# Block attention feeding a mixture of experts: keys scaled on GpSimd, TensorE's step grouped by kind of product, three PSUM banks each for scores and transposes

## The chip, the core and the metric

The kernel runs on one core of a Trainium2 chip. The metric is the device time of one execution in microseconds (us), given as the median of three runs. The profiler also recorded one execution with every instruction's start and duration; its span is counted from its first to its last instruction. In its rows PE is TensorE (PEld its weight loads), DVE is VectorE, ACT is ScalarE, POOL is GpSimd, and SPq is the queue on which SyncE issues DMA transfers.

## What is computed

Two stages follow each other. The first is attention with a window and block summaries (4 batches, 8 heads, 768 rows, head size 64), the second a mixture of 8 experts with the best two of them for each of the 3072 rows. Cut from the reference:

```python
k_sum = k.reshape(B, H, nb, block, D).max(axis=3)      # block 32: 24 summaries
v_sum = v.reshape(B, H, nb, block, D).mean(axis=3)
scores_l = scale * np.matmul(q, k.transpose(0, 1, 3, 2))   # scale = 1/8
scores_l_m = np.where(np.abs(pos[:, None] - pos[None, :]) < 16, scores_l, -1e9)
scores_s = scale * np.einsum('bhsd,bhnd->bhsn', q, k_sum) + np.log(block)
a = softmax(concatenate([scores_l_m, scores_s]))           # maximum taken off first
x = a @ concatenate([v, v_sum])                            # then [3072, 512]
noisy = x @ w_gate + log1p(exp(x @ w_noise)) * noise       # best two experts, softmax
out[row] += weight * (relu(x[row] @ w1[e]) @ w2[e])
```

## The kernel before

Attention goes over 24 tiles of 128 query rows (4 batches of 6 tiles; `t` is the tile). A tile's 128 rows are two blocks of 64, and each block needs 96 window keys plus the 24 block maxima, 120 keys in all. The 8 heads of a tile are split by partition half: `a` is the half (0 or 1), `hp` the four heads in it. The names of a tile's stages are:

- `kx_local` (L125) and `kx_sum` (L130): GpSimd copies the window keys (two copies of 128x384) and the block maxima into `kx`, the keys that TensorE reads. For the first tile `first_keys` (L238, L240) does this head by head.
- `mask_sums` (L315): four matmuls put the mask into the score tile `s`, and `scores` (L325): 32 matmuls add the products of `q` and `kx` to it. `s` has 2 buffers of 2 PSUM banks each, one bank for each half `a`.
- `smax` (L332): VectorE takes the maximum of each row and head. ScalarE makes its negative eighth, `nm` (L337), in a small copy.
- `sexp` (L339): eight exponentials on ScalarE, one for each head, four for each half `a`, with `nm` as bias and 0.125 as scale. The result is `p`.
- `p_trans` (L345): TensorE transposes `p`, four heads into each of the 2 banks `pt`; ScalarE copies each bank to `pts` (L348).
- `av` (L358): 32 matmuls of `pts` with the values give `o`; `norm` (L367, L371, L373) divides on VectorE and gives `x`.
- `x_pe` (L395): four transposes of `x` into `pt`, copied by ScalarE to `xt` (L401). `norm_hi` (L380, ScalarE) and `norm_lo` (L387, GpSimd) split `x` into two f16 parts that go to DRAM (`xd`).

The loop `for t in range(-2, NT - 1)` writes the instructions out in a pipelined order, and each engine works through its own list in that order. One turn holds the scores of tile t+2, the transposes of `p` of tile t+1, the `av` of tile t and the `x` of tile t-1. Some turns carry more: sums of the values (L266), the gate's products (L413, L424, L484 and on, L593), transfers, weight conversions (L686, L688). At a change of batch there is also the reduction of the keys to maxima (L231). Waits between engines are semaphore waits that the language derives from which tile each instruction reads and writes; the program that is built shows on which instruction each of them stands.

After the last tile (about 140 us into the span) the experts run: two large products (L871, L990), which fill TensorE to the end.

Of the kernel before, what the change touches and what calls it, by code (L numbers as in the profile page):

```python
# [20 lines left out]
P = 128  # L21
# [36 lines left out]
BIG = 1.5 * 2 ** 23  # L58


@with_exitstack
def attn_moe(ctx, tc, qt, kt, vt, wgn, noise, w1, w2, out):
# [10 lines left out]
    pairs = spair.enter_context(tc.tile_pool(name="pairs", bufs=2, space=PSUM))  # L73
# [45 lines left out]
    def kx_local(t):  # L119
        b, j = divmod(t, TS)  # L120
        for blk in range(2):
            c = j * P + 64 * blk
            r = max(0, c + W - S)
            k = KB[b % 2][:, r:r + HP * S].rearrange("p (h s) -> p h s", h=HP)
            nc.gpsimd.tensor_copy(KX[t % QN][:, :, blk, 0:W], k[:, :, c - r:c - r + W])  # L125

    def kx_sum(t):
        b, j = divmod(t, TS)
        if j < QN:
            (nc.gpsimd if b else nc.vector).tensor_copy(KX[t % QN][:, :, :, W:NK],  # L130
                                                        KM[b][:, :, None, :].to_broadcast([P, HP, 2, NB]))
# [102 lines left out]
    def first_keys():  # L234
        for h in range(HP):
            k = KB[0][:, h * S:]
            for blk in range(2):
                nc.gpsimd.tensor_copy(KX[0][:, h, blk, 0:W], k[:, 64 * blk:64 * blk + W])  # L238
            k_piece(0, h, 2 if h == HP - 1 else 1)
            nc.vector.tensor_copy(KX[0][:, h, :, W:NK], KM[0][:, h, None, :].to_broadcast([P, 2, NB]))  # L240
# [9 lines left out]
    C4 = 2 * (D + 1)  # L250

# [48 lines left out]
    SC, PE_, PT, PO, X, XR, XT = {}, {}, {}, {}, {}, {}, {}  # L300

    def gate_space():
        return pairs.tile([P, 2, 512], F32, name="s")
# [4 lines left out]
    def mask_sums(t):  # L308
        j = t % TS
        s = SC[t] = gate_space()[:, :, :SK].rearrange("p a (h k) -> p a h k", h=HP)  # L310
        for blk in range(2):
            for a in range(2):
                r = slice(64 * a, 64 * a + 64)
                m = masks[1 if (j, blk) == (0, 0) else 2 if (j, blk) == (TS - 1, 1) else 0]
                nc.tensor.matmul(s[64 * blk:64 * blk + 64, a, :, 0:W], identb[r, r],  # L315
                                 m[r, None, :].to_broadcast([64, HP, W]), start=True, stop=False,
                                 skip_group_check=True)

    def scores(t):
        s, q, k = SC[t], QR[t], KX[t % QN]  # L320
        for hp in range(HP):
            for blk in range(2):
                for a in range(2):
                    d = slice(64 * a, 64 * a + 64)
                    nc.tensor.matmul(s[64 * blk:64 * blk + 64, a, hp, :], q[d, hp, blk], k[d, hp, blk, :], start=False,  # L325
                                     stop=hp == HP - 1, skip_group_check=True)
# [3 lines left out]
    def smax(t):  # L330
        NM[t] = work.tile([P, 2, 2, HP], F32, name="nm", bufs=2)
        nc.vector.tensor_reduce(NM[t][:, 0], SC[t], axis=AX.X, op=OP.max)  # L332

    def sexp(t, a):
        if a == 0:
            PE_[t] = work.tile([P, 2, HP, NK], F32, name="p")
            nc.scalar.activation(NM[t][:, 1], NM[t][:, 0], AF.Copy, scale=-0.125)  # L337
        for hp in range(HP):
            nc.scalar.activation(PE_[t][:, a, hp, :], SC[t][:, a, hp, :], AF.Exp, bias=NM[t][:, 1, a, hp:hp + 1],  # L339
                                 scale=0.125)  # L340

    def p_trans(t, a):
        pt = psum.tile([P, HP, P], F32, name="pt", bufs=2)
# [6 lines left out]
    def av_space(t):  # L350
        PO[t] = outp.tile([P, 2, 512], F32, name="o") if t < NT - 2 else gate_space()
# [40 lines left out]
    def x_pe(t):  # L392
        pt = psum.tile([P, DC, P], F32, name="pt", bufs=2)
# [740 lines left out]
    mask_sums(0)  # L1134
    for t in range(-2, NT - 1):
# [9 lines left out]
        if t + 2 < NT:  # L1145
            scores(t + 2)
# [10 lines left out]
        if t + 3 < NT:  # L1157
            mask_sums(t + 3)
# [44 lines left out]

    spair.close()
# [294 lines left out]
```

## Time and profile before

| what | value |
|---|---|
| median of 3 runs | 659.58 us (657.78 to 660.11) |
| the profiled execution's own time | 656.8 us |
| its span | 655.0 us |
| granted TensorE clock, mean | 0.999 |
| PE busy | 634.5 us (97%) |
| DVE busy | 482.1 us (74%) |
| POOL busy | 330.8 us (51%) |
| ACT busy | 317.4 us (48%) |

The own time is 1.8 us above the span (launch and end), and 2.8 us below the median. Busy shares are means over both stages; the attention stage is about a fifth of the span. A row's duration of a matmul holds the drain of the pipeline, so the next row can start before it ends; the spacing from one start to the next tells what an instruction cost there.

### The profile page before, as it was taken

To read this page: it belongs to the slowest core of one execution; us is meant where nothing else is said; L and a number is where in the kernel's file an instruction comes from. 1 tells how busy PE (TensorE), PEld (TensorE's weight loads), DVE (VectorE), ACT (ScalarE), POOL (GpSimd) and SP (SyncE) were. 2 spreads that over 40 slices of the span, in tenths; PEclk is the share of its full clock that TensorE was granted. 3 is DMA by queue.
4 is the path that set the end of the run, shared out by engine and by line. 5 is a ranking of instruction groups with operands and counts; after the bars stand their busy time and mean duration, and the time that the engine had idled before them with its cause. 6 is when DMAs were issued, how large, how long until landed. Compare 5 with 4: busy or idle time off the path is not lost.

```text
span 655.0 us, 14037 instructions
## 1 busy us (share of the span) xinstructions
PE 634.5 (97%) x5407; PEld 369.9 (56%) x5407; DVE 482.1 (74%) x866; ACT 317.4 (48%) x677; POOL 330.8 (51%) x473
## 2 busy tenths in 40 slices
PE   8999899889999999999999999999999999999996
PEld 7777777665455554555455446544654555455543
DVE  6768989887597789587957894788678777856511
ACT  4879989752342563265326523542454155315300
POOL 5455545542846548563856375545556451632042
PEclk9999999999999999999999999999999999999999
DMA  9999998799988675546646674558257723431031
GB/s 307 317 318 353 310 336 248 217 299 336 257 167 164 237 193 153 202 130 191 167 156 185 160 202 158 171 163 230 95 192 164 238 68 115 144 127 49 1 110 41
DMA packets 104567, 125.62 MB, mean 192 GB/s; under 512 B 58393, under 2 KB 59681, under 8 KB 104492
## 3 DMA queue, kind: packets, MB, share of 16 engines
q1 hardware_dynamic: 92348, 88.37, 46.5%
q0 software_dynamic: 12144, 36.28, 17.4%
q8 instruction: 44, 0.72, 0.5%
q14 instruction: 31, 0.25, 0.1%
HBM read 87.38 MB, written 26.21 MB: 173 GB/s over the span
## 4 chain that ended last, share of the span: by engine, by line
PE 89%; ACT 5%; DVE 2%; issue 1%; POOL 1%; DMA 1%; POOLq 0%; DVEq 0%
PE pt L990 37%; PE h L871 26%; PE h L835 5%; PE a L871 4%; PE pt L987 3%; ACT p L339 2%; PE s L325 2%; PE o L358 2%; PE pt L345 2%; PE pt L395 1%; PE o L247 1%; ACT pts L348 1%; DMA htl<-htl 1%; PE pt L413 1%; PE h L990 1%
## 5 line engine op out<-in xcount | busy, mean ns | idle before, releaser
L93 POOL DMA_INDIRECT out_dram<-y,tb x48 | 65.4, 1362 | 150.6 <-DVE y L1013 140.6
L990 PEld LDWEIGHTS <-hth 128*128 128x128 f16 x768 | 74.9, 98 | 89.1
L990 PE MATMUL pt<-w2h,hth 128*128 128x512 f16 x376 | 88.8, 379 | 0.0
L990 PE MATMUL pt<-w2h,htl 128*128 128x512 f16 x376 | 88.8, 379 | 0.0
L990 PE MATMUL pt<-w2l,hth 128*128 128x512 f16 x376 | 88.8, 379 | 0.0
L93 POOL DMA_INDIRECT xg<-xd,tb x53 | 71.0, 1339 | 33.6 <-DVE oc L610 17.3
L871 PE MATMUL h<-tx,sh 128*128 128x402 f16 x336 | 77.8, 333 | 0.0
L1013 DVE SCALAR_TENSOR_TENSOR y<-pt,tb,prev 128x512 f32<-128x512 f32 x42 | 31.4, 749 | 52.5 <-PE pt L990 52.5
L693 DVE SCALAR_TENSOR_TENSOR w2l<-stg,w2h 128x1024 f16<-128x1024 f32 x32 | 49.1, 1543 | 27.8 <-ACT w2h L676 26.4
L990 PEld LDWEIGHTS <-htl 128*128 128x128 f16 x384 | 37.6, 98 | 45.3
L871 PEld LDWEIGHTS <-w1h 128*128 128x128 f16 x448 | 43.1, 97 | 33.0 <-issue 1.4
L387 POOL TENSOR_TENSOR xr<-x,xr 128x512 f16<-128x512 f32 x24 | 30.9, 1289 | 57.7 <-ACT xr L380 38.6
L93 POOL DMA_INDIRECT prev<-out_dram,tb x42 | 51.9, 1237 | 13.6 <-issue 13.6
L740 POOL TENSOR_TENSOR t<-xte 128x804 f32<-128x804 f16 x24 | 38.9, 1648 | 36.6 <-DVE t L696 31.1
L871 PE MATMUL h<-xte,w1h 128*128 128x402 f16 x224 | 56.3, 333 | 0.0
L339 ACT ACTIVATE p<-s,nm 128x120 f32<-128x120 f32 x192 | 53.7, 378 | 0.8
L893 ACT ACTIVATE p<-h 128x402 f32<-128x402 f32 x28 | 14.2, 507 | 74.0 <-issue 54.5
L768 ACT ACTIVATE tx<-t 128x804 f16<-128x804 f32 x28 | 23.7, 869 | 50.4 <-DVE t L696 50.4
L871 PEld LDWEIGHTS <-sh 128*128 128x128 f16 x336 | 32.6, 97 | 24.8
L871 PE MATMUL h<-tx,sl 128*128 128x402 f16 x168 | 42.2, 332 | 0.0
L721 ACT ACTIVATE sh<-ws 128x1536 f16<-128x1536 f32 x14 | 20.8, 1482 | 38.1 <-DVE ws L696 34.1
L879 DVE SCALAR_TENSOR_TENSOR htl<-h,hth 128x402 f16<-128x402 f32 x56 | 31.8, 569 | 8.4 <-ACT hth L876 8.3
(217 smaller groups left out, 1228.4 us busy)
## 6 DMA issues: line engine op xcount, KB each, us to landing
stg<-in_w_dram SPq DMA_DIRECT2D x62, 512.0 KB
q<-in_qt_dram SPq DMA_DIRECT2D x24, 256.0 KB
hth<-in_vt_dram SPq DMA_DIRECT2D x8, 768.0 KB
xd<-xr SPq DMA_DIRECT2D x24, 256.0 KB
out_dram<-prev SPq DMA_DIRECT2D x8, 768.0 KB
kb<-in_kt_dram SPq DMA_DIRECT2D x6, 768.0 KB
htl<-in_vt_dram SPq DMA_DIRECT2D x12, 260.0 KB
vw<-in_vt_dram SPq DMA_DIRECT2D x12, 260.0 KB
```

Source lines behind the costliest of these rows:

```text
L93: return nc.gpsimd.indirect_dma_start(**kw)
L339: nc.scalar.activation(PE_[t][:, a, hp, :], SC[t][:, a, hp, :], AF.Exp, bias=NM[t][:, 1, a, hp:hp + 1], scale=0.125)
L387: engine.tensor_tensor(XR[t][:, DM:], X[t], XR[t][:, 0:DM], op=OP.subtract)
L693: nc.vector.scalar_tensor_tensor(lo, SG[e, i], sc, hi, op0=OP.mult, op1=OP.subtract)
L721: nc.scalar.activation(h, x, AF.Copy, scale=W1S)
L740: nc.gpsimd.tensor_tensor(tt(e, 0 if low else j), xb(e, *i, low), xb(e, *o, low), op=OP.subtract)
L768: nc.scalar.activation(TX[e][:, 0, j - 1], t_of(e, j), AF.Copy)
L835: nc.tensor.matmul(ph[:, :n], w[wn][:, c, f * P:(f + 1) * P], x[:, xo + c, c0:c1], start=(k == 0), stop=(k == 11), skip_group_check=hook i ...
L871: nc.tensor.matmul(o, lhs[a][:, c], rhs[b][:, c], start=start and n == 0, stop=stop and n == 5, skip_group_check=True)
L879: nc.vector.scalar_tensor_tensor(HT[1][:, f, c0:c1], c, 0.0, HT[0][:, f, c0:c1], op0=OP.max, op1=OP.subtract)
L990: nc.tensor.matmul(py, hx[:, f, c * P:c * P + P], w[:, f, :], start=first, stop=final, skip_group_check=True)
L1013: nc.vector.scalar_tensor_tensor(y, py[:, :d], gw, pv[:, :d], op0=OP.mult, op1=OP.add)
```

## The change

Five things are changed in the attention stage.

1. The factor 1/8 goes into the keys: the copies into `kx` (L125, L130, L238, L240) become multiplications by `SCALE`, on the same engines.
2. `smax` writes the maximum negated, the copy L337 is gone, and the exponentials have no scale.
3. The scores lie in one tile `SB` of three banks: half 0 of every tile in bank 0, half 1 in bank 1 for even tiles and in bank 2 for odd ones. The mask of tile t+2 stands directly ahead of the scores of t+2, half 1 first.
4. TensorE's turn is ordered mask, scores, transposes of `p`, transposes of `x`, then all 32 `av` matmuls. The copy to `xt` stands behind all eight exponentials.
5. Transposes and other small products rotate over three banks (two `pt`, one `pt3`).

```diff
-                nc.gpsimd.tensor_copy(KX[t % QN][:, :, blk, 0:W], k[:, :, c - r:c - r + W])
+                nc.gpsimd.tensor_scalar(KX[t % QN][:, :, blk, 0:W], k[:, :, c - r:c - r + W], SCALE, None, op0=OP.mult)
...
+    def pt_space():
+        turn.append(len(turn) % 3 if attn_on else 0)
+        return pairs.tile([P, 512], F32, name="pt3") if turn[-1] == 2 else psum.tile([P, 512], F32, name="pt", bufs=2)
...
-        return pairs.tile([P, 2, 512], F32, name="s")
+    SB = pairs.tile([P, 3, 512], F32, name="s")
+
+    def s_bank(t, a):
+        return SB[:, a * (1 + t % 2), :SK].rearrange("p (h k) -> p h k", h=HP)
...
-        s = SC[t] = gate_space()[:, :, :SK].rearrange("p a (h k) -> p a h k", h=HP)
-        for blk in range(2):
-            for a in range(2):
+        SC[t] = SB[:, 0:2 + t % 2:1 + t % 2, :SK].rearrange("p a (h k) -> p a h k", h=HP)
+        for a in (1, 0):
+            s = s_bank(t, a)
+            for blk in range(2):
...
-        nc.vector.tensor_reduce(NM[t][:, 0], SC[t], axis=AX.X, op=OP.max)
+        nc.vector.tensor_reduce(NM[t], SC[t], axis=AX.X, op=OP.max, negate=True)
...
-            nc.scalar.activation(NM[t][:, 1], NM[t][:, 0], AF.Copy, scale=-0.125)
         for hp in range(HP):
-            nc.scalar.activation(PE_[t][:, a, hp, :], SC[t][:, a, hp, :], AF.Exp, bias=NM[t][:, 1, a, hp:hp + 1],
-                                 scale=0.125)
+            nc.scalar.activation(PE_[t][:, a, hp, :], s_bank(t, a)[:, hp, :], AF.Exp, bias=NM[t][:, a, hp:hp + 1])
...
         if t + 2 < NT:
+            mask_sums(t + 2)
             scores(t + 2)
...
-        if t + 3 < NT:
-            mask_sums(t + 3)
+        if t >= 1:
+            x_pe(t - 1)
...
-            av(t, range(H // 2))
-        if t >= 1:
-            x_pe(t - 1)
-        run(t + 0.09)
         run(t + 0.3)
         run(t + 0.32)
-        if t >= 1:
-            x_copy(t - 1)
+        if t >= 0:
+            av(t)
         if t + 2 < NT:
             sexp(t + 2, 1)
         if t >= 1:
+            if t != NT - 4:
+                x_copy(t - 1)
             norm_hi(t - 1)
             norm_lo(t - 1)
-        if t >= 0:
-            av(t, range(H // 2, H))
```

How this moves instructions is seen in the built programs, where a row is one instruction (or a number of like ones) of one engine in its order, and the brackets name the engines on which it waits. The first place is TensorE's turn in the middle of batch 0, before the change: scores, transposes of `p`, mask of the next tile, half of `av`, transposes of `x`, the other half.

```order
L325 MATMUL s<-kx_95,q_101 64x120 [waits DMAHW5_49,Pool_49]
L325 MATMUL s<-kx_95,q_101 64x120 [waits Pool_49]
L345 MATMUL pt<-ident,p 120x128 [waits PE_49,Activation_49]
L345 MATMUL pt<-ident,p 120x128 [waits Activation_49] x3
L315 LDWEIGHTS identb
L315 MATMUL s<-mask_122,identb 64x4x96 [waits DVE_49]
...
L358 MATMUL o<-htl,pts 64x65 [waits DMAHW0_49,DMAHW7_49,DVE_49,PE_49]
L358 MATMUL o<-htl,pts 64x65 x7
L395 MATMUL pt<-ident,x 128x128 [waits Activation_49]
L395 MATMUL pt<-ident,x 128x128 x3
L358 MATMUL o<-htl,pts 64x65 x8
```

The same turn after the change (mask L327, scores L337, transposes of `p` L355, of `x` L405, `av` L368):

```order
L327 LDWEIGHTS identb [waits DVE_49]
L327 MATMUL s<-mask_122,identb 64x4x96 [waits Activation_49]
...
L337 MATMUL s<-kx_95,q_101 64x120 [waits DMAHW5_49,Pool_49]
L337 MATMUL s<-kx_95,q_101 64x120 [waits Pool_49]
L355 MATMUL pt<-ident,p 120x128 [waits PE_49]
L355 MATMUL pt<-ident,p 120x128 x3
L355 MATMUL pt_613<-ident,p 120x128 [waits PE_49]
L405 MATMUL pt<-ident,x 128x128 [waits DVE_49,Activation_49]
L405 MATMUL pt<-ident,x 128x128 x3
L368 MATMUL o<-htl,pts 64x65 [waits DMAHW7_49,DMAHW0_49,PE_49]
L368 MATMUL o<-htl,pts 64x65 x15
```

The wait on ScalarE, which every transpose of `p` had, now stands on the first mask matmul of the tile, the one into half 1; the transposes and the scores between have none of their own.

The second place is the head of TensorE's list, from the scores of tile 1 on. Before, with the scores of tile 1 (`kx_95`) and 2 (`kx_96`):

```order
L315 MATMUL s<-mask_122,identb 64x4x96
L325 MATMUL s<-kx_95,q_98 64x120 [waits DMAHW6_49,DVE_49,Pool_49]
L325 MATMUL s<-kx_95,q_98 64x120 x13
L345 MATMUL pt<-ident,p 120x128 [waits Activation_49] x8
L315 LDWEIGHTS identb
L315 MATMUL s<-mask_122,identb 64x4x96 [waits DVE_49]
...
L325 MATMUL s<-kx_96,q_99 64x120 [waits DMAHW7_49,DVE_49,Pool_49]
```

After:

```order
L327 LDWEIGHTS identb [waits DVE_49]
L327 MATMUL s<-mask_122,identb 64x4x96 [waits Activation_49]
...
L337 MATMUL s<-kx_95,q_98 64x120 [waits DMAHW6_49,Pool_49]
L337 MATMUL s<-kx_95,q_98 64x120 x13
L355 MATMUL pt<-ident,p 120x128 x8
L327 LDWEIGHTS identb [waits DVE_49]
L327 MATMUL s<-mask_122,identb 64x4x96 [waits Activation_49]
...
L337 MATMUL s<-kx_96,q_99 64x120 [waits DMAHW7_49,Pool_49]
```

Here too the waits on ScalarE moved from the transposes to the mask that stands ahead of the scores, and the mask and scores of tile 1 stand behind such a wait, where none stood before.

The third place is ScalarE's turn. Before, with the copy L337 and the copy to `xt` (L401) between the two groups of exponentials:

```order
L348 ACTIVATE pts<-pt 120x512 [waits PE_49] x2
L337 ACTIVATE nm<-nm 128x8 [waits DVE_49]
L339 ACTIVATE p<-s,nm 128x120 [waits Activation_49]
L339 ACTIVATE p<-s,nm 128x120 x3
L401 ACTIVATE xt<-pt 128x512 [waits PE_49]
L339 ACTIVATE p<-s,nm 128x120 x4
L380 ACTIVATE xr<-x 128x512
```

After:

```order
L358 ACTIVATE pts<-pt 120x512 [waits PE_49,Activation_49]
L358 ACTIVATE pts<-pt_701 120x512 [waits PE_49]
L350 ACTIVATE p<-s,nm 128x120 [waits DVE_49]
L350 ACTIVATE p<-s,nm 128x120 x7
L411 ACTIVATE xt<-pt 128x512 [waits PE_49]
L390 ACTIVATE xr<-x 128x512
```

All eight exponentials now stand together, and the copies to `xt` and `xr` behind them.

## Rows read from the trace of the kernel before

**Rows 1.** Windows by stage: us, busy us of each engine (instructions), granted clock, DMA share, GB/s.

```profile
0.00:20.00 20.00, 16.99 (x298) 14.24 (x298) 13.04 (x37) 9.59 (x31) 11.43 (x43) 1.00 0.95 304
20.00:50.00 30.00, 27.83 (x561) 22.34 (x561) 19.72 (x32) 24.39 (x78) 13.63 (x22) 1.00 1.04 320
50.00:130.00 80.00, 74.52 (x1475) 59.44 (x1469) 72.30 (x225) 70.98 (x221) 41.53 (x59) 1.00 0.93 295
140.00:170.00 30.00, 30.00 (x195) 17.13 (x193) 21.87 (x70) 8.20 (x16) 11.80 (x19) 1.00 0.97 326
180.00:640.00 460.00, 460.00 (x2635) 241.20 (x2634) 340.32 (x462) 191.12 (x312) 235.30 (x308) 1.00 0.53 154
```

The engines' columns are in the order PE, PEld, DVE, ACT, POOL.

**Rows 2.** Timeline, a turn without extra work: start, duration, engine, line, instructions [idle before].

```profile
24.72 1.05 PE L325 MATMUL s<-kx,q 64*64 64x120 f32 x32
25.70 1.09 PE L345 MATMUL pt<-ident,p 128*120 128x128 f32 x8
26.46 1.14 ACT L348 ACTIVATE pts<-pt 120x512 f32<-120x512 f32 x2
26.72 0.36 PE L315 MATMUL s<-mask,identb 64*64 64x384 bf16 x4
27.41 0.28 ACT L337 ACTIVATE nm<-nm 128x8 f32<-128x8 f32 x1
27.62 0.66 PE L395 MATMUL pt<-ident,x 128*128 128x128 f32 x4
27.73 1.12 ACT L339 ACTIVATE p<-s,nm 128x120 f32<-128x120 f32 x4
28.21 0.69 PE L358 MATMUL o<-htl,pts 120*64 120x65 f32 x16
28.83 1.05 PE L325 MATMUL s<-kx,q 64*64 64x120 f32 x32
30.69 1.15 ACT L348 ACTIVATE pts<-pt 120x512 f32<-120x512 f32 x2
```

**Rows 3.** Timeline of the start, columns as in the group above.

```profile
8.51 0.36 PE L315 MATMUL s<-mask,identb 64*64 64x384 bf16 x4
8.70 1.06 PE L325 MATMUL s<-kx,q 64*64 64x120 f32 x32
9.79 1.05 PE L325 MATMUL s<-kx,q 64*64 64x120 f32 x32
9.84 1.16 DVE L332 TENSOR_REDUCE nm<-s 128x8 f32<-128x960 f32 x1
11.27 2.12 ACT L339 ACTIVATE p<-s,nm 128x120 f32<-128x120 f32 x8
11.68 2.09 PE L345 MATMUL pt<-ident,p 128*120 128x128 f32 x8 [0.84 <-ACT p L339]
13.89 0.99 PE L325 MATMUL s<-kx,q 64*64 64x120 f32 x32
14.53 2.13 ACT L339 ACTIVATE p<-s,nm 128x120 f32<-128x120 f32 x8
14.81 1.80 PE L266 MATMUL o<-hth 128*24 128x130 f32 x48
16.53 1.09 PE L345 MATMUL pt<-ident,p 128*120 128x128 f32 x8
17.22 1.09 ACT L348 ACTIVATE pts<-pt 120x512 f32<-120x512 f32 x2 [0.56 <-PE pt L345]
```

**Rows 4.** Timeline, scores (L325) of tiles 3 and 23, first and last of 21.

```profile
20.61 1.05 PE L325 MATMUL s<-kx,q 64*64 64x120 f32 x32 [1.10 <-POOL htl L284]
126.20 1.05 PE L325 MATMUL s<-kx,q 64*64 64x120 f32 x32
```

**Rows 5.** POOL's groups in the first 12 us: instructions, busy us, mean ns.

```profile
L125 POOL COPY kx<-kb 128x384 f32<-128x384 f32 x6 | 2.8, 515 | 0.0
L196 POOL TENSOR_SCALAR iotar<-iotar 128x128 f16<-128x128 f16 x1 | 0.5, 529 | 0.1
```

More of the change, by code (lines that the diff above doesn't have):

```diff
@@ L58 @@
 BIG = 1.5 * 2 ** 23
+SCALE = D ** -0.5
 @with_exitstack
@@ L129, in kx_sum @@
         if j < QN:
-            (nc.gpsimd if b else nc.vector).tensor_copy(KX[t % QN][:, :, :, W:NK],
-                                                        KM[b][:, :, None, :].to_broadcast([P, HP, 2, NB]))
+            (nc.gpsimd if b else nc.vector).tensor_scalar(KX[t % QN][:, :, :, W:NK],
+                                                          KM[b][:, :, None, :].to_broadcast([P, HP, 2, NB]),
+                                                          SCALE, None, op0=OP.mult)
     def q_piece(t):
@@ L250, in attn_moe @@
     C4 = 2 * (D + 1)
+    turn = []
+    def pt_space():
+        turn.append(len(turn) % 3 if attn_on else 0)
+        return pairs.tile([P, 512], F32, name="pt3") if turn[-1] == 2 else psum.tile([P, 512], F32, name="pt", bufs=2)
+    attn_on = [1]
     PV = {}
@@ L259, in v_sums_pe @@
         if b:
-            pt = psum.tile([P, HP, P], F32, name="pt", bufs=2).rearrange("p a b -> p (a b)")
+            pt = pt_space()
         else:
@@ L309, in mask_sums @@
         j = t % TS
-        s = SC[t] = gate_space()[:, :, :SK].rearrange("p a (h k) -> p a h k", h=HP)
-        for blk in range(2):
-            for a in range(2):
+        SC[t] = SB[:, 0:2 + t % 2:1 + t % 2, :SK].rearrange("p a (h k) -> p a h k", h=HP)
+        for a in (1, 0):
+            s = s_bank(t, a)
+            for blk in range(2):
                 r = slice(64 * a, 64 * a + 64)
                 m = masks[1 if (j, blk) == (0, 0) else 2 if (j, blk) == (TS - 1, 1) else 0]
-                nc.tensor.matmul(s[64 * blk:64 * blk + 64, a, :, 0:W], identb[r, r],
+                nc.tensor.matmul(s[64 * blk:64 * blk + 64, :, 0:W], identb[r, r],
                                  m[r, None, :].to_broadcast([64, HP, W]), start=True, stop=False,
@@ L319, in scores @@
     def scores(t):
-        s, q, k = SC[t], QR[t], KX[t % QN]
+        s, q, k = [s_bank(t, a) for a in range(2)], QR[t], KX[t % QN]
         for hp in range(HP):
@@ L324, in scores @@
                     d = slice(64 * a, 64 * a + 64)
-                    nc.tensor.matmul(s[64 * blk:64 * blk + 64, a, hp, :], q[d, hp, blk], k[d, hp, blk, :], start=False,
+                    nc.tensor.matmul(s[a][64 * blk:64 * blk + 64, hp, :], q[d, hp, blk], k[d, hp, blk, :], start=False,
                                      stop=hp == HP - 1, skip_group_check=True)
@@ L330, in smax @@
     def smax(t):
-        NM[t] = work.tile([P, 2, 2, HP], F32, name="nm", bufs=2)
-        nc.vector.tensor_reduce(NM[t][:, 0], SC[t], axis=AX.X, op=OP.max)
+        NM[t] = work.tile([P, 2, HP], F32, name="nm", bufs=2)
+        nc.vector.tensor_reduce(NM[t], SC[t], axis=AX.X, op=OP.max, negate=True)
     def sexp(t, a):
@@ L336, in sexp @@
             PE_[t] = work.tile([P, 2, HP, NK], F32, name="p")
-            nc.scalar.activation(NM[t][:, 1], NM[t][:, 0], AF.Copy, scale=-0.125)
         for hp in range(HP):
-            nc.scalar.activation(PE_[t][:, a, hp, :], SC[t][:, a, hp, :], AF.Exp, bias=NM[t][:, 1, a, hp:hp + 1],
-                                 scale=0.125)
+            nc.scalar.activation(PE_[t][:, a, hp, :], s_bank(t, a)[:, hp, :], AF.Exp, bias=NM[t][:, a, hp:hp + 1])
     def p_trans(t, a):
-        pt = psum.tile([P, HP, P], F32, name="pt", bufs=2)
+        pt = pt_space().rearrange("p (a b) -> p a b", a=HP)
         for hp in range(HP):
@@ L350, in av_space @@
     def av_space(t):
-        PO[t] = outp.tile([P, 2, 512], F32, name="o") if t < NT - 2 else gate_space()
+        PO[t] = outp.tile([P, 2, 512], F32, name="o") if t < NT - 1 else SB[:, 0:2]
     def av(t, hs=range(H)):
@@ L392, in x_pe @@
     def x_pe(t):
-        pt = psum.tile([P, DC, P], F32, name="pt", bufs=2)
+        pt = pt_space().rearrange("p (a b) -> p a b", a=DC)
         for c in range(DC):
@@ L409, in gate_gt @@
         t0 = GN * b
-        pt = psum.tile([P, HP, P], F32, name="pt", bufs=2)[:, 0]
+        pt = pt_space()[:, :P]
         for c in range(DC):
@@ L422, in gate_gl @@
     def gate_gl(b):
-        pt = psum.tile([P, HP, P], F32, name="pt", bufs=2)[:, 0]
+        pt = pt_space()[:, :P]
         nc.tensor.transpose(pt, LT[b], ident)
@@ L1132, in attn_moe @@
     DVE_HI = (4, 5, 8, 10)
-    mask_sums(0)
     for t in range(-2, NT - 1):
@@ L1156, in attn_moe @@
             p_trans(t + 1, 1)
-        if t + 3 < NT:
-            mask_sums(t + 3)
+        if t >= 1:
+            x_pe(t - 1)
+        run(t + 0.09)
+        if t == NT - 4:
+            x_copy(t - 1)
         if t + 2 < NT:
@@ L1202, in attn_moe @@
         PREV.append(x)
+    attn_on.clear()
     spair.close()
```

9 lines of the change are left out of this document (5 added, 4 removed).

## The prediction

> **What bounds the kernel now.** I read the busy time by stage first. The experts fill TensorE: 30.00 of 30 us between 140 and 170, and 460.00 of 460 later [rows 1]. Nothing in that stage is edited, so what the attention stage gains or loses reaches the end nearly unchanged. In the attention stage TensorE is busy for 27.83 of 30 us and then 74.52 of 80, and from 50 us on VectorE (72.30) and ScalarE (70.98) are close behind [rows 1]. Three engines are near their limits there, so a saving on one is worth little by itself.
>
> Then the timeline of a turn without extra work. The scores of successive tiles start at 24.72 and 28.83, that is 4.11 us apart, and no row of TensorE in between names idle time: TensorE's list sets the turn. ScalarE takes 4.23 (26.46 to 30.69) and falls behind a little [rows 2]. The engines overlap because a tile's scores (28.83) are computed while ScalarE still takes exponentials of the tile before: that tile has another buffer of `s`.
>
> Over the stage, the scores of 21 tiles start between 20.61 and 126.20, in twenty spacings of 5.28 on average [rows 4]. Nine of them are 4.11 to 4.67 (39.2 us in sum), three 4.97 to 5.12 (15.1), and eight, with value sums or gate products in them, 5.70 to 7.03 (51.3).
>
> **The change, part by part.**
>
> *Fewer changes of kind on TensorE.* Eight transposes of `p` take 1.02 (25.70 to 26.72), four of `x` 0.59 (27.62 to 28.21) [rows 2]. That is 0.1075 for a transpose and 0.16 for the start of a block. Before, a turn has six blocks (scores, `p`, mask, half `av`, `x`, half `av`); after, mask and scores join, `x` follows `p`, and `av` is whole: three. That saves 3 x 0.16 = 0.48, and TensorE's list of a plain turn falls from 4.11 to 3.63. [...]
>
> *The copy `nm` goes.* From its start to the exponentials is 0.32 (27.41 to 27.73) [rows 2], so ScalarE's turn falls to 3.91. With both savings alone a turn would be about 3.95.
>
> *The wait on the mask.* This decides. The order shows that every transpose of `p` waited on ScalarE before, and that none does afterwards, though each still reads what the exponentials write. A wait can only be left off if an earlier instruction of TensorE's list has already waited for the same point. The only such instruction is the first mask matmul of the next tile, which writes half 1, a bank that the preceding tile doesn't use. So this mask waits for the last of the preceding tile's eight exponentials, four of which read half 1 in the other bank: three banks of one tile don't act as three buffers. Since TensorE takes its list in order, the scores, transposes and `av` behind the mask wait as well. Now tile after tile goes round one closed chain:
>
> - mask to scores: 0.19 (8.51 to 8.70) [rows 3];
> - scores to the first transpose of `p`: 0.93 (0.98 from 24.72 to 25.70 [rows 2], less 0.05, since 13.89 to 14.81 is 0.92 [rows 3]);
> - first transpose to the copy `pts`: 0.69 (16.53 to 17.22) [rows 3];
> - two copies: 0.95 to 0.98 (26.46 to 27.41 [rows 2] gives 0.95; I take 0.97);
> - eight exponentials: 2.13 [rows 3], where four take 1.12 [rows 2], so 0.25 for each further one and 0.37 for the first;
> - from ScalarE to TensorE: 0.05 (the first exponential ends 0.37 after 11.27, the transposes start at 11.68 [rows 3]).
>
> The sum is 4.96 us for a turn. The branch by way of the maximum is shorter: 1.14 from the scores to L332 and 1.16 for it [rows 3], 2.30, against 0.93 + 0.69 + 0.97 = 2.59. It stays hidden with 0.3 to spare. Transposes and copies of `x`, `av`, L380 and L401 fit beside: TensorE has 3.63 of work for the 4.96, ScalarE 3.91.
>
> *The start.* Before, the scores of tile 1 start at 9.79, while tile 0 is still being reduced, and those of tile 2 at 13.89 [rows 3]. After, the maximum of tile 0 ends at 11.00 as before, its exponentials run from 11.05 to 13.18, the mask of tile 1 goes at 13.23 and its scores at 13.42. Transposes of tile 0 start at 14.35, the copies at 15.04, the exponentials of tile 1 run from 16.01 to 18.14, and the scores of tile 2 start at 18.38. Behind them stand the sums of the values (1.72, 14.81 to 16.53 [rows 3]), to 21.03. Then transposes, copies at 21.72, exponentials of tile 2 from 22.69 to 24.82, and the scores of tile 3 at 25.06, where they were at 20.61 [rows 4]: **+4.45**. The row of 20.61 names POOL's L284 as its releaser, which follows the sums of the values; these end 4.5 later, so this way gives the same.
>
> *The twenty turns from there.* Nine short ones go from 39.2 to 9 x 4.96 = 44.6, **+5.5**. Three go from 15.1 to 14.9, **-0.2**. In the eight long ones TensorE's extra work fills the time in which it would wait: they can win 0.48 each (3.8), and 1.5 more where TensorE stood still in one of them for an unnamed reason. VectorE, busy for 90% [rows 1], lets less through. I take **-4.5**, between 0 and -5.3. In sum **+0.8**. Behind the last tile the missing copy and two block starts give **-0.3**.
>
> *Multiplying on GpSimd.* The copy of 128x384 takes 515 ns; the only multiplication on GpSimd is of 128x128 f16, 529 ns [rows 5]. A multiplication of 384 then lies between 0.52 and 3 x 0.53 = 1.59 us; I take 0.8, since the small one also has a fixed part. GpSimd works 41.53 of 80 us [rows 1], 2.74 in a turn of 5.28. Two multiplications add 0.6 to that, up to 2.1: its list stays under 4.96 and costs nothing but for the head, where up to 0.3 of the first keys lies ahead of the first scores. If the turn were 3.95 it would count. [...]
>
> *Third bank for transposes, copy `xt` last.* TensorE's transposes no longer wait for the copies; TensorE now has 1.3 of slack in a turn, which hides this. Nothing.
>
> *The sum:* 4.45 + 0.8 - 0.3 = +4.95. The span goes from 655.0 to 660.0, the own time of 656.8 to 661.8, and by the same difference of 2.8 the median from 659.58 to about **664.5**. All rows show the clock at 1.00 in the attention stage [rows 1]. [...]
>
> **Rivals.**
>
> 1. *The mask waits by bank* (ends on the other side). If the wait only ends with the four exponentials of half 0, a turn is 4.96 - 4 x 0.25 = 3.96, the start gives +1.5 (three waits, each 1.0 shorter), and the nine short turns fall to 35.6 (-3.6); VectorE's share in the long ones lets through 0 to -4.5. Sum about -3: 656.5. For it speaks the diff, which gives each half its own bank. Against it stands the order: transposes without a wait need the last exponential behind the mask. It decides as soon as TensorE's mask starts more than 0.5 us before the last exponential's end. Chance 0.10.
> 2. *GpSimd becomes the bound.* With 1.59 a product, its turn is 2.74 + 2.14 = 4.9, and its waits for L380 come on top; at 0.4 in each of twenty turns this adds 8: 672. It needs the upper bound. Chance 0.06.
> 3. *TensorE's saving comes through.* 20 x 0.48 = 9.6 less, and no start lost: 650. It needs TensorE alone as the bound, which the 72.30 and 70.98 of 80 [rows 1] and the wait speak against. Chance 0.03.
> 4. *The turn is soft.* VectorE's slow turns hold back neighbours and the short ones ahead catch up on them; with queued work in buffers, of the +5.5 only half is lost, and the long ones win their 4.5: +2 in all, 661.5. The start speaks against a smaller number, since its 4.45 has no neighbour to catch up with. Chance 0.21.
>
> **How the numbers follow.** The forecast (a closed chain at 4.96, start lost) has 0.60. Its own range is 662 to 669: the long turns may give nothing (+4.5), or 5.3 instead of 4.5 (-0.8); the head of GpSimd +0.3; the clock +2. Leaving out the two ends at 650 and 672 and half of rival 1, the range is 657.5 to 669. About 0.5%, 3.3 us, is what a measurement of this kernel tells from no change: faster is under 656.3, slower over 662.9. Rival 1 is faster in two cases of three (0.07), rival 3 always: 0.10. Rival 4 (0.21), the rest of rival 1 (0.03) and 0.01 of the forecast lie within: 0.25. The other 0.59 of the forecast and rival 2 are slower: 0.65.
>
> **What would show it.** In the changed profile the first mask (L327) of a tile should start 0.05 after the end of the eighth exponential (L350), with ScalarE as the releaser of TensorE's idle time in the short turns, about 1 us a turn. Scores (L337) of the tiles 1, 2 and 3 should start near 13.4, 18.4 and 25.1, short turns should take 4.96, and the first expert matmul (L881 where L871 was) should come 5 us later. A mask that starts while the exponentials still run makes the forecast wrong, and so does a plain turn under 4.5. The GpSimd group L126 should show 0.6 to 1.0 us a product; TensorE's transposes of `x` should lose their 0.16.

## The result, and the profile after

The changed kernel takes 666.64 us (median of 4 runs, 665.3 to 667.18) against 659.25 for the kernel before: a ratio of 1.0113, 95% interval 1.008 to 1.0145. Measured again beside the kernel before (experiment 9) it was 1.0152 (1.0113 to 1.0192). It is slower, by 7.4 us, where 4.9 was forecast; 666.64 lies in the range of 657.5 to 669. The profiled execution's span went from 655.0 to 664.7, so 9.7 us more, and its own time from 656.8 to 666.48.

A turn without extra work first, in the timeline of the changed kernel (start, duration, engine, line, idle before), which answers to [rows 2]:

```profile
34.39 0.36 PE L327 MATMUL s<-mask,identb 64*64 64x384 bf16 x4 [1.29 <-ACT p L350]
34.56 1.01 PE L337 MATMUL s<-kx,q 64*64 64x120 f32 x32
35.50 1.09 PE L355 MATMUL pt<-ident,p 128*120 128x128 f32 x8
36.25 1.09 ACT L358 ACTIVATE pts<-pt 120x512 f32<-120x512 f32 x2 [0.90 <-PE pt L355]
36.43 0.60 PE L405 MATMUL pt<-ident,x 128*128 128x128 f32 x4
36.56 2.30 POOL L126 TENSOR_SCALAR kx<-kb 128x384 f32<-128x384 f32 x2
36.96 1.15 PE L368 MATMUL o<-htl,pts 120*64 120x65 f32 x32
37.22 2.13 ACT L350 ACTIVATE p<-s,nm 128x120 f32<-128x120 f32 x8
39.40 0.36 PE L327 MATMUL s<-mask,identb 64*64 64x384 bf16 x4 [1.29 <-ACT p L350]
```

The chain is closed: the mask, the scores, the transposes, two copies, eight exponentials, and 0.05 after their end (37.22 + 2.13 = 39.35) the mask of the next tile at 39.40. The turn is 39.40 - 34.39 = 5.01 us, where it was 4.11. TensorE stands idle for 1.29 of it, with the exponentials as releaser. TensorE's own work in the turn is 5.01 - 1.29 = 3.72 (4.11 before, 3.63 forecast): most of the saving of the block starts is there, and it ends up in the idle time. The transposes of `x` cost 0.53 (36.43 to 36.96) instead of 0.59, so they lost 0.06 and not the 0.16 that the prediction named.

The chain of waits on TensorE from 14 to 138 us has this as its first row (engine and line <- released by: us in total, times, longest):

```profile
PE s L327 <- ACT p L350: 17.8, 14, 3.5
PE s L327 <- DVE ixf L475: 1.8, 1, 1.8
PE s L327 <- DVE x L383: 1.6, 2, 1.3
```

The start, timeline of the changed kernel, which answers to [rows 3, 4]:

```profile
7.32 0.95 DVE L233 TENSOR_REDUCE kmax<-kb 128x24 f32<-128x768 f32 x1 [0.86 <-DMA kb<-in_kt_dram]
10.13 0.43 PE L337 MATMUL s<-kx,q 64*64 64x120 f32 x8 [0.86 <-DVE kx L242]
10.65 1.16 DVE L344 TENSOR_REDUCE nm<-s 128x8 f32<-128x960 f32 x1 [0.50 <-PE s L337]
14.02 0.54 PE L327 MATMUL s<-mask,identb 64*64 64x384 bf16 x4 [3.45 <-ACT p L350]
14.29 1.86 PE L337 MATMUL s<-kx,q 64*64 64x120 f32 x32
16.08 1.96 PE L355 MATMUL pt<-ident,p 128*120 128x128 f32 x8
20.74 0.54 PE L327 MATMUL s<-mask,identb 64*64 64x384 bf16 x4 [2.70 <-ACT p L350]
21.01 1.86 PE L337 MATMUL s<-kx,q 64*64 64x120 f32 x32
29.54 1.01 PE L337 MATMUL s<-kx,q 64*64 64x120 f32 x32
```

The scores of tile 1 begin at 14.29 (9.79 before), of tile 2 at 21.01 (13.89) and of tile 3 at 29.54 (20.61). From 14 us on a block of scores takes 1.79 from its start to the next block's, nearly twice the 0.94 of later. Windows of 2 us show the clock meanwhile (us, busy us of PE, PEld, DVE, ACT, POOL with instructions, granted clock, DMA share, GB/s):

```profile
8.00:10.00 2.00, 1.27 (x35) 0.92 (x32) 1.92 (x6) 0.00 (x0) 2.00 (x5) 1.00 1.05 399
10.00:12.00 2.00, 0.43 (x8) 0.36 (x9) 1.50 (x3) 0.16 (x1) 2.00 (x3) 0.95 1.08 416
12.00:14.00 2.00, 0.00 (x0) 0.00 (x0) 0.33 (x1) 1.97 (x8) 2.00 (x3) 0.50 1.06 352
22.00:24.00 2.00, 2.00 (x44) 1.53 (x40) 0.96 (x1) 0.00 (x0) 0.00 (x0) 0.50 1.08 396
24.00:26.00 2.00, 2.00 (x36) 1.45 (x29) 0.48 (x2) 0.00 (x0) 0.00 (x0) 0.63 0.29 107
26.00:28.00 2.00, 1.52 (x26) 1.14 (x26) 1.31 (x4) 1.77 (x6) 0.95 (x2) 1.00 0.00 0
```

TensorE waits 3.45 us for the exponentials of tile 0; in that gap the granted clock goes to 0.50, and comes back between 24 and 26 us.

So of the 9.7 us the start makes 8.93 (29.54 - 20.61). The twenty spacings that follow end with the scores of tile 23 at 135.66, that is 106.12 us against 105.59: +0.53. What is left, 0.24, lies behind.

The multiplications on GpSimd, in its groups (instructions | busy us, mean ns), against [rows 5]:

```profile
L126 POOL TENSOR_SCALAR kx<-kb 128x384 f32<-128x384 f32 x46 | 54.3, 1200 | 0.1
```

### The profile page after: what moved, and what is told of

It reads as the page before. It is cut to its first block, busy times and chain, and to the rows that moved or that the text cites. A ratio compares the mean times of both kernels' runs of the same rounds, so it can differ in the third digit from the quotient of the medians.

```text
span 664.7 us, 14012 instructions
## 1 busy us (share of the span) xinstructions
PE 627.3 (94%) x5407; PEld 372.9 (56%) x5407; DVE 479.0 (72%) x866; ACT 313.7 (47%) x653; POOL 364.1 (55%) x473
## 4 chain that ended last, share of the span: by engine, by line
PE 85%; ACT 8%; DVE 3%; DMA 2%; issue 1%; SPq 0%; POOL 0%; POOLq 0%; DVEq 0%; ACTq 0%
PE pt L1000 37%; PE h L881 26%; ACT p L350 5%; PE h L845 4%; PE a L881 4%; PE pt L997 3%; PE s L337 3%; PE pt L355 2%; ACT pts L358 2%; PE o L368 1%; PE s L327 1%; DMA htl<-htl 1%; DMA kb<-in_kt_dram 1%; PE h L1000 1%; PE pt L405 1%
## 5 line engine op out<-in xcount | busy, mean ns | idle before, releaser
L350 ACT ACTIVATE p<-s,nm 128x120 f32<-128x120 f32 x192 | 51.1, 393 | 11.5 <-DVE nm L344 11.5
L126 POOL TENSOR_SCALAR kx<-kb 128x384 f32<-128x384 f32 x46 | 54.3, 1200 | 0.1
L397 POOL TENSOR_TENSOR xr<-x,xr 128x512 f16<-128x512 f32 x24 | 28.9, 1206 | 31.1 <-ACT xr L390 21.7
L344 DVE TENSOR_REDUCE nm<-s 128x8 f32<-128x960 f32 x24 | 27.7, 1156 | 23.2 <-PE s L337 21.5
```

The costliest lines, as they stand in the source:

```text
L126: nc.gpsimd.tensor_scalar(KX[t % QN][:, :, blk, 0:W], k[:, :, c - r:c - r + W], SCALE, None, op0=OP.mult)
L344: nc.vector.tensor_reduce(NM[t], SC[t], axis=AX.X, op=OP.max, negate=True)
L350: nc.scalar.activation(PE_[t][:, a, hp, :], s_bank(t, a)[:, hp, :], AF.Exp, bias=NM[t][:, a, hp:hp + 1])
L397: engine.tensor_tensor(XR[t][:, DM:], X[t], XR[t][:, 0:DM], op=OP.subtract)
```

## Experiments

Each ratio is to the kernel before, measured beside it, with its 95% interval. A trace is of one execution of each.

**1. The PSUM layout undone** (the pool `pairs` has two buffers again).

```diff
-    SB = pairs.tile([P, 3, 512], F32, name="s")
+    def gate_space():
+        return pairs.tile([P, 2, 512], F32, name="s")
...
-        turn.append(len(turn) % 3 if attn_on else 0)
-        return pairs.tile([P, 512], F32, name="pt3") if turn[-1] == 2 else psum.tile([P, 512], F32, name="pt", bufs=2)
+        return psum.tile([P, 512], F32, name="pt", bufs=2)
```

> The changed kernel with only its PSUM layout undone: scores in two buffers of two banks, transposes in two banks; the new order on TensorE, the multiplications on GpSimd and the negated maximum stay. Theory (the closed chain through the mask's wait on the last exponential, and the clock that falls in the gaps it makes at the start): the gaps between scores and masks go, the granted clock stays at 1.00 from 0 to 50 us, scores of tile 3 start at 20.6 to 22.5 instead of 29.5, short turns fall from 5.01 to between 4.0 and 4.6 (where GpSimd's two products and its rest end a turn), median 654 to 660. Rival (the multiplications on GpSimd, 1.15 us each, are what the change cost): GpSimd's list is as long as in the changed kernel, short turns stay near 5.0 and the median at 664 or more.

659.69 us, 1.0039 (1.0015 to 1.0064). The scores of tile 3 start at 20.58, the first two turns from there take 4.12, the clock from 0 to 50 us is 1.00. Then GpSimd is late, in the timeline and the waits of this kernel (14 to 138 us):

```profile
29.85 1.09 PE L337 MATMUL s<-kx,q 64*64 64x120 f32 x28 [0.67 <-POOL kx L126]
```

```profile
PE s L337 <- POOL kx L126: 3.6, 7, 0.7
```

The layout thus makes most of the loss: with it 1.0113 and 1.0152, without it 1.0039, as the theory said. The edit takes away the third bank of transposes along with the one score tile; experiment 2 tells them apart. What remains goes with GpSimd's multiplications (experiments 4 and 5).

**2. A tile for each score bank.** The maximum is taken in two reductions; at the end one normalisation stands ahead of the last `av`.

```diff
-    SB = pairs.tile([P, 3, 512], F32, name="s")
+    SB = [pairs.tile([P, 512], F32, name=f"s{i}") for i in range(3)]
...
-        nc.vector.tensor_reduce(NM[t], SC[t], axis=AX.X, op=OP.max, negate=True)
+        for a in range(2):
+            nc.vector.tensor_reduce(NM[t][:, a], s_bank(t, a), axis=AX.X, op=OP.max, negate=True)
```

> The changed kernel with its three score banks as three tiles, so that the mask of half 0 waits for the fourth exponential and that of half 1 for none of the preceding tile; the maximum is taken in two reductions, one for each half, and the last tile's normalisation order at the end is shifted. Theory (closed chain): the chain is 1.0 us shorter, short turns fall from 5.01 to 4.0 to 4.6, the idle gap of TensorE behind the first scores is 1 us shorter or more; median 656 to 661. If the clock still falls in the shorter gap at the start, 2 to 3 us of the loss stay: up to 663. Rival (GpSimd): as the changed kernel, 665 to 668, as the banks change nothing on GpSimd.

660.69 us, 1.0053 (1.0025 to 1.0082). The order of the built program now has no wait on the mask of half 1, and the wait for the fourth exponential on that of half 0. The timeline shows both:

```profile
27.00 2.13 ACT L350 ACTIVATE p<-s,nm 128x120 f32<-128x120 f32 x8
27.81 0.71 PE L326 MATMUL s<-mask,identb 64*64 64x384 bf16 x4
28.17 0.10 PEld L326 LDWEIGHTS <-identb 64*64 64x64 bf16 x1 [0.25 <-issue]
28.28 1.06 PE L336 MATMUL s<-kx,q 64*64 64x120 f32 x32
```

The mask begins in the midst of the exponentials and the turn is 3.93 (24.35 to 28.28). So it is the one tile over three banks that made the mask wait for the last exponential. The twenty spacings from tile 3 to tile 23 take 102.78 us in sum, 2.8 less than in the kernel before. The start takes more than that: the scores of tile 3 begin at 24.35 instead of 20.61, and the clock from 0 to 20 us is still 0.84.

**3. The scaling undone, the rest as changed** (parts 1 and 2 of the change, in all four copies).

```diff
-            nc.gpsimd.tensor_scalar(KX[t % QN][:, :, blk, 0:W], k[:, :, c - r:c - r + W], SCALE, None, op0=OP.mult)
+            nc.gpsimd.tensor_copy(KX[t % QN][:, :, blk, 0:W], k[:, :, c - r:c - r + W])
...
-        nc.vector.tensor_reduce(NM[t], SC[t], axis=AX.X, op=OP.max, negate=True)
+        nc.vector.tensor_reduce(NM[t][:, 0], SC[t], axis=AX.X, op=OP.max)
...
+            nc.scalar.activation(NM[t][:, 1], NM[t][:, 0], AF.Copy, scale=-0.125)
```

> The changed kernel with only its scaling undone: copies on GpSimd again, the small copy of the maximum and the scale of the exponentials back; PSUM layout and TensorE's order stay. Theory (closed chain): the copy of the maximum lies on the chain, so short turns go from 5.01 to about 5.3, scores of tile 3 start at 29.0 to 30.5 (0.8 less by GpSimd, 0.3 more by each of three copies), the clock still falls at the start, and the median stays at 665 to 671. Rival (GpSimd's multiplications are the cost): it falls to near the kernel before, 657 to 661.

668.29 us, 1.0166 (1.0139 to 1.0192). Short turns take 5.18: the copy of the maximum lies on the chain and costs 0.17 of the 0.3 expected. TensorE's waits:

```profile
PE s L325 <- ACT p L349: 26.7, 19, 3.7
```

GpSimd's multiplications are gone and nothing is won: the scores of tile 3 start at 28.73, 0.4 to 0.8 us earlier than in the changed kernel's two traces, and the copy of the maximum takes more than that. The rival that blames the multiplications falls for this kernel.

**4. The scaling alone, in the kernel before.**

```diff
-            nc.gpsimd.tensor_copy(KX[t % QN][:, :, blk, 0:W], k[:, :, c - r:c - r + W])
+            nc.gpsimd.tensor_scalar(KX[t % QN][:, :, blk, 0:W], k[:, :, c - r:c - r + W], SCALE, None, op0=OP.mult)
...
-            nc.scalar.activation(NM[t][:, 1], NM[t][:, 0], AF.Copy, scale=-0.125)
```

> The kernel before with only the scaling changed: multiplications on GpSimd, negated maximum, no small copy. Theory (closed chain is the main loss): TensorE stays the bound of short turns, with GpSimd's way from the split of x through two products to the scores now at about 4.6 in two-turn average, so short turns go from 4.11 to between 4.2 and 4.6; the first scores are 0.6 to 0.8 later; median 659 to 663. Rival (GpSimd): the whole loss, 665 to 668.

659.28 us, 1.003 (1.001 to 1.0049), in the theory's range; ScalarE's small copy is left out in it as well. Plain turns take 4.11 and 4.24, but TensorE waits for GpSimd:

```profile
PE s L328 <- POOL kx L126: 5.4, 8, 0.8
```

**5. The order alone** (TensorE's, with ScalarE's copy to `xt` behind the exponentials), which is experiment 1 with the edits of experiment 3 as well, so two buffers of scores and two banks of transposes; against the kernel before its loop differs like this (the moves of the copies aren't shown):

```diff
+            mask_sums(t + 2)
             scores(t + 2)
...
-            mask_sums(t + 3)
+            x_pe(t - 1)
...
-            av(t, range(H // 2))
+            av(t)
```

> The kernel before with only the new order on TensorE (mask, scores, transposes of p and of x, all av; copy to xt behind the exponentials; copies on GpSimd, small copy of the maximum, two buffers of scores as before). Theory (the order itself saves block starts on TensorE, but ScalarE's 4.23 a turn and VectorE take its place): short turns 4.2 to 4.3 instead of 4.11, the long ones up to 0.48 shorter, idle time of TensorE behind ScalarE; median 655 to 659, so 0 to 3 us under the kernel before. Rival (the saving of the block starts comes through): short turns 3.7 to 3.9, median 648 to 652. Against the two-buffer kernel with multiplications it gives what GpSimd's multiplications cost where nothing waits for the mask: 2 to 4 us.

656.56 us, 0.9985 (0.9968 to 1.0001): no difference that counts. Plain turns take 4.12 and 4.23, so the saved block starts don't show. The transposes of `x`, which stand right behind those of `p` now, wait for the copy `pts`, 0.25 in the turn of 4.12, so that TensorE's own work there is 3.87. From 20 to 132 us this wait is the first of TensorE's; in the kernel before it was 1.7 us, 4 times:

```profile
PE pt L405 <- ACT pts L358: 7.7, 21, 0.8
```

In the changed kernel, which has a third bank for transposes, TensorE's list of waits has no such row. Against experiment 1 the products on GpSimd cost 0.5%.

**6. The gaps at the start filled.** 36 and 28 matmuls into the third bank of transposes, results unused.

```diff
+    def keep_warm(n):
+        o = pairs.tile([P, 512], F32, name="pt3") if n else None
+        for i in range(n):
+            nc.tensor.matmul(o[:, 0:P], identb, identb, start=True, stop=True, skip_group_check=True)
...
+            if t < 1:
+                keep_warm((0, 36, 28)[t + 2])
             mask_sums(t + 2)
```

> The changed kernel with 36 and 28 matmuls of the identity (128x128, results unused) in the two gaps of TensorE ahead of the masks of tiles 1 and 2. Theory (of the start's 8.9 us, some 3.7 are the lower clock in the rows from 14 to 25 us): the granted clock stays at 1.00 to 30 us, scores of tile 1, 2 and 3 start at 14.0 to 14.5, 18.9 to 19.6 and 25.5 to 26.5 instead of 14.3, 21.0 and 29.5; short turns stay at 5.01; median 662 to 664. Rival (the clock costs nothing, since ScalarE and the waits set the start): scores of tile 3 stay at 29 or later, median 666 to 668.

663.31 us, 1.0106 (1.0084 to 1.0128). The clock is 1.00 from 0 to 50 us, and the scores of tiles 1, 2 and 3 start at 13.69, 18.63 and 25.04. From tile 1 to tile 3 that is 11.35 us, where the changed kernel has 15.25: the clock cost 3.9 there. (The scores of tile 1 are 0.6 earlier as well, but these start at 14.29 and 13.83 in two traces of the changed kernel itself.) Two turns from 70.46 on take 5.84 and 7.25, where the changed kernel has 5.34 and 5.46. The span is 3.6 us shorter than the changed kernel's; the ratio doesn't tell the two kernels apart.

**7. As experiment 5, the negative eighth of the maximum made by VectorE.**

```diff
-            nc.scalar.activation(NM[t][:, 1], NM[t][:, 0], AF.Copy, scale=-0.125)
+        nc.vector.tensor_scalar(NM[t][:, 1], NM[t][:, 0], -SCALE, None, op0=OP.mult)
```

> As the kernel with the order alone, but the negative eighth of the maximum (128x8) is made by VectorE behind its reduction instead of by ScalarE. Theory: ScalarE's turn falls from 4.23 to 3.92 and TensorE's is 3.8 with the wait for the copy pts; short turns 3.9 to 4.0; VectorE has 0.15 to 0.25 more in each turn and holds the long ones, which give part of it back. Median 653 to 657, the fastest of these kernels. Rival (VectorE is the limit already, so that its 24 extra instructions cost as much as ScalarE wins): 656 to 660, as the kernel before.

657.07 us, 1.0018 (0.9997 to 1.0039): the theory's size missed, the rival's holds. The same window of experiment 5, then of this kernel:

```profile
50.00:130.00 80.00, 70.33 (x1463) 58.43 (x1463) 70.61 (x218) 71.17 (x221) 37.95 (x52) 0.98 0.94 298
50.00:130.00 80.00, 69.31 (x1461) 56.77 (x1457) 73.75 (x232) 68.40 (x204) 38.63 (x57) 1.00 0.92 298
```

ScalarE has 2.8 us less to do, and VectorE 3.1 more; its small product takes 0.33 in the mean, where 0.15 to 0.25 was expected. The first two short turns are 4.12, not 3.9 to 4.0, since the transposes of `x` wait 0.25 for `pts` here too.

**8. Experiment 2 with the edits of experiment 3**, of which the reduction reads

```diff
-            nc.vector.tensor_reduce(NM[t][:, a], s_bank(t, a), axis=AX.X, op=OP.max, negate=True)
+            nc.vector.tensor_reduce(NM[t][:, 0, a], s_bank(t, a), axis=AX.X, op=OP.max)
```

> The kernel with one tile for each score bank, its scaling undone: copies on GpSimd, the small copy of the maximum back. Theory (with the mask waiting for the fourth exponential alone, a closed chain of 3.96 + 0.21 for the small copy remains, and GpSimd no longer ends a turn): short turns 4.2 to 4.3, the start still 1 to 3 us late with a lower clock for part of it; median 656 to 660. Rival (GpSimd's multiplications cost nothing there): 659 to 662, as with the multiplications.

660.83 us, 1.0052 (1.0032 to 1.0072), a miss by the theory; it lies in the rival's range, and experiment 2 has 1.0053. Short turns are 4.17 to 4.23 as expected, but the clock falls at the start (0.81 from 0 to 20 us, scores of tile 3 at 26.29) and, in the traced execution, again later (0.96 in the mean from 50 to 130 us, with turns of 8.15 and 7.12 from 78.60, in and behind a wait of 1.78 for the transfer of `htl`). That execution is the slowest of the six.

**9 to 11. The changed kernel again, with the gaps filled, and a version meant to be faster** (a tile for each bank, copies on GpSimd, the eighth on VectorE, 24 and 16 matmuls in the gaps), measured side by side. The second has the edit of experiment 6; the third is experiment 8 with those of 6 and 7, the numbers apart:

```diff
-                keep_warm((0, 36, 28)[t + 2])
+                keep_warm((0, 24, 16)[t + 2])
```

> The changed kernel itself, so that it stands beside the next two on one chip. Both theories: 1.010 to 1.014 of the kernel before; scores of tile 3 at 29 to 30 us, short turns 5.01.

> The changed kernel with 36 and 28 matmuls of the identity in the gaps ahead of the masks of tiles 1 and 2, as before. Theory (the lower clock at the start costs 3.7 to 4.5 us of the span): 3 to 5 us under the changed kernel in the same call, unless the granted clock falls later in its stead, which the windows would show. Rival (the time of the start is given back behind it, or the clock falls anyway): within 1.5 us of the changed kernel.

> One tile for each score bank, copies on GpSimd, the negative eighth of the maximum made by VectorE, and 24 and 16 matmuls of the identity in the gaps ahead of the masks of tiles 1 and 2: the layout of the change with each of the three found costs lessened. Theory: scores of tile 3 start at 22 to 23.5 us with the clock at 1.00, short turns 3.95 to 4.1; 1.5 to 2.5 us lost at the start against the kernel before, 2 to 4 won after it; median between 3 us under and 1 over the kernel before. Rival (VectorE holds the long turns, with two reductions and a small product more in each): 1 to 4 us over it.

The changed kernel: 667.74, 1.0152 (1.0113 to 1.0192); filled: 665.92, 1.0127 (1.0077 to 1.0176); the third: 664.45, 1.009 (1.0058 to 1.0122). By the medians the filled one is 1.8 us under the changed kernel, between what its theory and its rival said. In the traces it wins 3.7 us at the start (scores of tile 3 at 25.48 against 29.16; from tile 1 on 11.35 against 15.33) and loses it again, most of it in two turns from 70.85 on, 6.65 and 8.91. In the midst of the scores there, with no engine as releaser, its timeline has

```profile
81.00 0.67 PE L342 MATMUL s<-kx,q 64*64 64x120 f32 x6 [2.51 <-issue]
```

and behind this stop the clock is at 0.50 from 82 to 84 us. The third kernel does what was meant at the start (scores of tile 3 at 22.73, clock 1.00), but has five such stops of over 1 us up to 145 us:

```profile
44.45 0.64 PE L339 MATMUL s<-kx,q 64*64 64x120 f32 x16 [2.33 <-issue]
73.92 1.04 PE L373 MATMUL o<-vw,pts 120*64 120x65 f32 x28 [1.30 <-issue]
93.97 0.83 PE L339 MATMUL s<-kx,q 64*64 64x120 f32 x19 [1.66 <-issue]
103.13 0.95 PE L373 MATMUL o<-htl,pts 120*64 120x65 f32 x18 [2.27 <-issue]
142.76 1.15 PE L373 MATMUL o<-vw,pts 120*64 120x65 f32 x32 [1.46 <-issue]
```

Together these stand for 9.0 us. VectorE has a part in it too, in the early short turns, which take 4.49 and not 3.95 to 4.1: its two reductions and the small product lie on the chain, and ScalarE waits for them.

```profile
30.60 2.12 ACT L354 ACTIVATE p<-s,nm 128x120 f32<-128x120 f32 x8 [0.39 <-DVE nm L348]
```

The theory falls, and so does the rival, which held VectorE alone to account and said 1 to 4 us over the kernel before; it is 7.5.

**12. The gaps filled with fewer, wider matmuls** (14 and 10 over 512 columns), against experiment 6:

```diff
-        o = pairs.tile([P, 512], F32, name="pt3") if n else None
+        o = pairs.tile([P, 512], F32, name="pt3").rearrange("p (a b) -> p a b", a=4) if n else None
...
-            nc.tensor.matmul(o[:, 0:P], identb, identb, start=True, stop=True, skip_group_check=True)
+            nc.tensor.matmul(o, identb, identb[:, None, :].to_broadcast([P, 4, P]), start=True, stop=True, skip_group_check=True)
...
-                keep_warm((0, 36, 28)[t + 2])
+                keep_warm((0, 14, 10)[t + 2])
```

> The changed kernel with 14 and 10 matmuls of the identity over 512 columns in the gaps ahead of the masks of tiles 1 and 2, instead of 36 and 28 over 128: the same gaps filled with 24 matmuls and not 64, so that what follows stands 80 rows earlier in TensorE's list. Theory (the lower clock at the start costs 3.7 to 4.5 us, and what the other two fillings gave back at 72 to 86 us comes from a stop of TensorE in the midst of like matmuls that lies at another place of the list here): clock 1.00 to 30 us, scores of tile 3 at 25 to 26.5 us, no turn over 7.5 us with a lower clock behind it, 1.004 to 1.009 of the kernel before. Rival (the gain of the start is always given back): 1.010 to 1.014, as the changed kernel.

664.92 us, 1.0105 (1.0074 to 1.0135). The clock is 1.00 in all stretches to 640 us and the scores of tile 3 start at 25.57. No turn is over 7 us, but those from 60.70, 87.99 and 94.56 take 5.97, 6.57 and 6.02 (5.28, 5.49 and 5.11 in the changed kernel), with stops of 0.37, 0.88 and 0.82 of the same kind. The scores of tile 23 start at 134.12, only 1.5 earlier than in the changed kernel, and the span is 0.8 shorter. The theory is right on the start, and a clock at 1.00 where the stops are shorter fits what it says of the second fall; on the total 1.0105 lies in the rival's range, with an interval that reaches into both. In the traces, then, most of the start's gain is given back here and in experiment 10, but only 0.9 of 4.5 us in experiment 6; the filled kernels' ratios of 1.0105 to 1.0127 against 1.0113 and 1.0152 don't settle how much of it stays.

## Why the prediction was right, and what it mis-sized

*The wait on the mask* was read from the order and came out as said: 0.05 behind the eighth exponential, a turn of 5.01 for the 4.96 worked out. Experiment 2 shows the cause, since three tiles let the mask go after the fourth exponential; experiment 1 shows the price of the layout, the start with its clock included, 0.7 to 1.1% of the time; experiment 3 shows that what is laid on the chain lengthens every turn.

*The saved block starts* were rightly held to be hidden behind the wait; in a turn they measure 0.39 where 0.48 was worked out. That they are worth nothing without the wait is not shown. With two banks for transposes (experiment 5) the wait for `pts` and ScalarE's turn put the time back to 4.12 to 4.23; with three banks and a tile for each score bank (experiment 2) short turns reach 3.93 and the twenty spacings are 2.8 us shorter than before, which the start uses up.

*The twenty turns* were put at +0.8 and measured +0.53, but in parts that make up for each other: the nine short ones take 6.9 us more where 5.5 was forecast, the eight long ones 6.2 less, beyond the 5.3 that were held possible.

*The start* is the term that was mis-sized: 4.45 forecast, 8.93 measured. Up to the scores of tile 1 it was 0.87 too short (14.29 for 13.42), from there to tile 3 3.61 (15.25 for 11.64). The second part is the clock, which fell in the first gap: with the gaps filled, the same stretch takes 11.35 to 11.36 (experiments 6, 10 and 12), so the clock cost 3.9 to 4.0 us. The sum had nothing for it. The range allowed 0 to 2, an amount that no run shows: the rows ahead of the prediction have the clock at 1.00 throughout the attention stage [rows 1], and the runs then showed it at 0.50, with those 3.9 to 4.0 us. The rest of the walk held. The first part is mostly the maximum of tile 0, which starts at 10.65 instead of 9.84. How much of that GpSimd's products of the first keys make is not shown: TensorE's last wait there names VectorE's L242, whose maxima had waited 0.86 for the keys' transfer, and the same maximum starts at 10.19 in the changed kernel's other trace, and at 10.34 and 10.62 with copies on GpSimd (experiments 3 and 5).

*The total* has luck in it. The span was forecast to grow by 4.95 and grew by 9.7. The forecast of the median then carried over the 2.8 us by which the kernel before's median lay above its traced execution; for the changed kernel this is 0.16 (666.64 against 666.48). With 2.8 again the median would have been 669.3, just past the end of the range. Nor do the allowances named for that range add up to it: taken together they run from 663.7 to 671.3. Of the signs that were named, the mask's wait of 0.05 and the turn near 4.96 came true; the scores of tiles 1 to 3, the first expert matmul (9.6 us later, not 5), GpSimd's product and the 0.16 of the transposes of `x` did not.

*GpSimd's product* was taken at 0.8 us, between 0.52 and 1.59, and is 1.16 at the shortest and 1.20 in the mean, past the 0.6 to 1.0 of the signs: 46 of them make 54.3 us. Under a closed chain of 5.01 it stayed hidden once the start was over, as argued; without the chain it costs 0.3% (experiment 4) to 0.5% (experiment 1 against 5). The copy takes 515 ns [rows 5] and the multiplication of the same shape 1200.

No version tried beats the kernel before by more than its uncertainty; the order alone, at 0.9985, comes nearest.

## What to carry to other kernels

Banks were buffers here only as separate tiles (a turn of 3.93 us, against 5.01 with one tile over all three): where one tile holds several, read from the built program on which instruction the wait stands, and walk the chain that it closes. When a wait disappears from a row of an engine's order and the data are still needed, look for the earlier row that covers it: all between the two now waits as well. A gap of TensorE costs more than its length if the clock falls in it, here 3.9 us on top, and a multiplication put in the place of a copy on GpSimd more than doubled that instruction (515 to 1200 ns). When a forecast goes from a trace to a median, the distance between the two is itself a guess.

## What the runs showed of the hardware

The clock fell in a gap of 3.45 us, with 1.27 of 2 us of work before it, and stayed at 0.50 for about 13.7 us (the windows from 10 to 26 us added up), over 2 us windows with TensorE fully busy among them. The turns with 1.29 us of idle time in 5.01, such as the one from 34.39 to 39.40, kept it at 1.00.

The stops without a releaser were not expected. In the kernel before there is one, in the midst of `av`:

```profile
43.25 0.45 PE L358 MATMUL o<-htl,pts 120*64 120x65 f32 x7 [1.56 <-issue]
```

Its DMA queues from 40.6 to 41.9 us (packets, MB, share of 16 engines), and those of experiment 10 from 78.3 to 79.6, each hold one packet on the queue that the profile calls `instruction`, among the data:

```profile
q1 hardware_dynamic: 235, 0.42, 96.5%
q8 instruction: 1, 0.02, 5.8%
```

```profile
q1 hardware_dynamic: 254, 0.46, 97.6%
q8 instruction: 1, 0.02, 5.5%
```

TensorE starts again 1.42 and 1.52 us after the ends of these packets. The changed kernel's trace has two such stops, of 1.04 us before 100.39 and of 0.53 us before 107.68, and they end 1.28 and 1.32 us after the end of a packet on q8.

In these traces the place of a stop goes with TensorE's list. Experiments 5 and 7, which differ only in the engine that makes the negative eighth, have their first three of over 0.3 us in the same places, with 34 sums of the values, 20 scores and 20 `av` of a block still to come (16.85, 30.68 and 39.56 us in the one; 16.22, 30.07 and 38.84 in the other). Experiments 6 and 10 run the same kernel, and both stop ahead of the last 6 scores of the same tile (78.98 and 81.00). Their lengths do not go with the list: 0.62, 0.62 and 1.39 us in experiment 5 against 0.35, 0.75 and 1.39 in 7, and 1.69 us in experiment 6 against 2.51 in 10, which has another of 0.90 ahead of that. So two traces of one kernel differ by 1.7 us in these stops. What TensorE waits for in them, and whether the packets on q8 end them, is not shown.
